# Splitting two loads of x so that the last store of a one-core attention-and-MLP kernel takes another DMA semaphore

## Chip, cores, metric

The kernel runs on one core of one Trainium2 chip. The metric is the device time of one execution in microseconds (us). The experiments e1 to e4 ran on one chip, e5 to e8 on another, each beside the kernel before.

## The reference, cut to what matters

```python
def reference(x, state, moe_w_in, moe_w_out):          # x [8,8,512,64], state [8,8,32,64]
    scores = 0.125 * x @ state^T;  xread = softmax(scores) @ state
    scores2 = 0.125 * state @ x^T; sread = softmax(scores2) @ x
    t = concat([xread, sread], axis=2) -> [4352, 512]  # 8 batches of 544 rows, heads side by side
    h = t @ moe_w_in                                   # 512 -> 2048
    return (h * sigmoid(h)) @ moe_w_out                # 2048 -> 512, float32
```

## The kernel before

x comes in batch by batch into two buffers in turn. x(4) to x(7) are loaded on the SP queue in the main loop, one load of 1 MB each, long before they are used:

```python
    def load_x(b, h0=0, nh=H, eng=nc.gpsimd):
        eng.dma_start(
            x_f[b % 2][:, ds(h0, nh)],
            x[b, ds(h0, nh)].rearrange("h (p c) d -> p h c d", p=128, c=4)
        )
    # ...
    for b in range(1, B):
        n = b + 1
        m = n + 1
        # ...
                if m + 1 < B:
                    if at == (0, 2):
                        load_x(m + 1, eng=nc.sync)
                    if at == (1, 0):
                        for c in range(4):
                            cast_x(m + 1, nc.gpsimd, c, 1)
                    if at == (2, 10):
                        transpose_x(m + 1)
```

The last 128 rows to be computed are written in pieces, so that the last one is small:

```python
    def last_cols(b, tt, f, n, eng, queue):
        # ... sixteen matmuls into ps, then
        o = opool.tile([128, n], FP32, tag=f"o_part{f}", name="o_part")
        copy(eng, o[:], ps[:, 0:n])
        queue.dma_start(out_sread[ds(512, 32), ds(4 * tt, 4), cols], o[:])
    # ...
    last_cols(B, 1, 0, 256, nc.scalar, nc.sync)
    last_cols(B, 1, 256, 128, nc.vector, nc.scalar)
    last_cols(B, 1, 384, 128, nc.vector, nc.sync)
```

What the source does not show: the framework gives the DMAs issued by SP and ScalarE eight semaphores in turn, HW0 to HW7, in program order. At the end of the program SP checks all of them, one instruction after the other, in a fixed order. In the built program of the kernel before that end reads so (SW0 to SW7 are the semaphores of GpSimd's DMAs; what each check waits for is in brackets):

```
check SW7, SW6
check HW0, SW5
check HW1, SW4
check HW2, SW3        [128 rows x 512, last but three]
check HW3, SW2        [last piece, columns 0-255]
check HW4, SW1        [last piece, columns 256-383, issued by ScalarE]
check HW5, SW0        [last piece, columns 384-511: the very last store]
check HW6, VectorE
check HW7, ScalarE
drain (GpSimd)
drain, barrier of all engines (twice), end
```

The softmax here doesn't subtract the row's maximum and nothing guards it: scores larger than these inputs give would overflow.

## Time and profile before

| | kernel before |
|---|---|
| time, median of three | 212.74 us (212.74 to 212.76) |
| profiled execution: time, span of its records | 213.31 us, 211.54 us |
| TensorE busy | 203.7 us, 96% |
| last store: issued, landed (last of the 16 increments of its semaphore) | 208.605, 210.505 us |
| from that landing to the end of the span | 1.035 us |

The span ends with the last record; the time is longer than the span by a nearly constant 1.77 to 1.82 us in the profiled executions compared here. The profiled execution is slower by 0.57 us than the three that were timed. To see where in the span time lies, take three stretches: up to 18.75 us, then 189.50 us up to the end of the matmuls, then the rest. The view of busy time by stretches, kernel before (columns: stretch, its length, then busy us and count of instructions for TensorE, its weight loads, VectorE, ScalarE and GpSimd, then granted clock, DMA share, GB/s):

```profile
0.00:18.75 18.75, 15.83 (x122) 6.99 (x124) 10.32 (x29) 11.37 (x23) 13.12 (x25) 1.00 1.07 198
18.75:208.25 189.50, 187.91 (x1430) 89.83 (x1451) 63.52 (x116) 127.98 (x221) 26.93 (x38) 1.00 0.51 130
208.25:211.54 3.29, 0.00 (x0) 0.00 (x0) 0.29 (x1) 0.00 (x0) 0.00 (x0) 1.00 0.22 69
```

TensorE fills the long middle. In the last 3.29 us no engine computes but VectorE for 0.29 us: there the time is copy, store, landing and the end of the program.

### The profile page before, as it was taken

To read this page: it belongs to the slowest core of one execution; us is meant where nothing else is said; L and a number is where in the kernel's file an instruction comes from. 1 tells how busy PE (TensorE), PEld (TensorE's weight loads), DVE (VectorE), ACT (ScalarE), POOL (GpSimd) and SP (SyncE) were. 2 spreads that over 40 slices of the span, in tenths; PEclk is the share of its full clock that TensorE was granted. 3 is DMA by queue.
4 is the path that set the end of the run, shared out by engine and by line. 5 is a ranking of instruction groups with operands and counts; after the bars stand their busy time and mean duration, and the time that the engine had idled before them with its cause. 6 is when DMAs were issued, how large, how long until landed. Compare 5 with 4: busy or idle time off the path is not lost.

```text
span 211.5 us, 3841 instructions
## 1 busy us (share of the span) xinstructions
PE 203.7 (96%) x1550; PEld 96.8 (46%) x1575; DVE 74.1 (35%) x146; ACT 139.3 (66%) x244; POOL 40.1 (19%) x62
## 2 busy tenths in 40 slices
PE   7799999999999999999999999999999999999993
PEld 2444454444444444444444444444444444466653
DVE  3842257657841236113410653043412306100011
ACT  3866677899577867697569855996775166644410
POOL 8672215503320042012201202000200000000000
PEclk9999999999999999999999999999999999999999
DMA  6999999995549756555935429114221111011112
GB/s 196 193 203 207 287 258 340 226 272 179 103 104 239 205 130 138 122 176 102 233 80 183 104 64 207 50 53 99 80 69 37 63 64 53 0 50 50 53 50 99
DMA packets 42929, 28.65 MB, mean 135 GB/s; under 512 B 28064, under 2 KB 37792, under 8 KB 42912
## 3 DMA queue, kind: packets, MB, share of 16 engines
q1 hardware_dynamic: 36720, 20.65, 37.4%
q0 software_dynamic: 5904, 7.64, 17.4%
q8 instruction: 12, 0.20, 0.4%
q10 hardware_dynamic: 288, 0.13, 0.2%
q14 instruction: 5, 0.04, 0.1%
HBM read 17.43 MB, written 8.91 MB: 125 GB/s over the span
## 4 chain that ended last, share of the span: by engine, by line
PE 90%; DMA 5%; POOL 2%; issue 1%; DVE 0%; POOLq 0%
PE o L566 50%; PE h L525 25%; DMA w_in_sb<-in_moe_w_in_dram 5%; PE ps_w L469 4%; PE h L546 3%; PE o_a L566 3%; PE o_part L588 2%; PE ps_sr L416 1%; PE ps_scT L332 1%; POOL w_in_sb L150 1%; POOL w_out_sb L153 1%; PE ps_sc L306 0%; PE ps_xt L253 0%; DVE W L159 0%; POOL st_n L191 0%
## 5 line engine op out<-in xcount | busy, mean ns | idle before, releaser
L566 PE MATMUL o<-w_out_sb,g 128*128 128x512 bf16 x480 | 129.5, 379 | 1.3 <-issue 0.5
L557 ACT ACTIVATE g<-h 128x512 bf16<-128x512 f32 (+1 forms) x143 | 81.3, 573 | 34.1 <-PE h L525 19.9
L566 PEld LDWEIGHTS <-g 128*128 128x128 bf16 x528 | 50.3, 98 | 59.1 <-issue 3.8
L525 PE MATMUL h<-aT,W 128*128 128x512 bf16 x247 | 73.1, 379 | 0.1
L159 DVE COPY o_sb<-o 128x512 f32<-128x512 f32 x15 | 10.4, 691 | 89.1 <-PE o L566 86.2
L525 PEld LDWEIGHTS <-W 128*128 128x128 bf16 x254 | 24.5, 98 | 30.3 <-issue 0.7
L159 DVE CAST W<-ps_w 128x512 bf16<-128x512 f32 (+2 forms) x36 | 22.2, 658 | 23.2 <-PE ps_w L469 23.2
L157 ACT ACTIVATE W<-ps_w 128x512 bf16<-128x512 f32 (+1 forms) x32 | 16.2, 562 | 11.1 <-PE ps_w L469 11.1
L159 POOL CAST x_nat<-x_f 128x512 bf16<-128x512 f32 x24 | 14.7, 655 | 35.7 <-DMA x_f<-in_x_dram 35.7
L157 ACT ACTIVATE o_sb<-o 128x512 f32<-128x512 f32 x16 | 9.5, 597 | 14.4 <-PE o L566 11.9
L362 POOL TENSOR_TENSOR an<-e,rcn 128x512 bf16<-128x512 bf16 x5 | 7.6, 1517 | 48.0 <-DVE rcn L360 48.0
L469 PE MATMUL ps_w<-w_in_sb,stT 64*32 64x512 bf16 (+2 forms) x264 | 10.3, 373 | 0.6 <-DMA w_in_sb<-in_moe_w_in_dram 0.6
L566 PE MATMUL o_a<-w_out_sb,g 128*128 128x512 bf16 x31 | 9.8, 379 | 0.2
L546 PE MATMUL h<-xmT,w_in_sb 128*128 128x256 bf16 x64 | 9.6, 273 | 0.1
L546 PEld LDWEIGHTS <-w_in_sb 128*128 128x128 bf16 x64 | 6.3, 98 | 3.9
L359 DVE TENSOR_REDUCE rs<-e 128x32 f32<-128x1024 bf16 x5 | 6.1, 1213 | 3.1 <-DMA e<-eT 3.1
L165 PE MATMUL ps_busy<-busy 128*128 128x512 bf16 x15 | 5.9, 497 | 1.2 <-DVE warm L172 1.2
L346 ACT ACTIVATE eT<-ps_scT 128x512 bf16<-128x512 f32 x10 | 5.4, 597 | 1.6 <-PE ps_scT L332 1.6
L786 ACT ACT_TABLE_LOAD x5 | 6.4, 1283 | 0.1
L469 PEld LDWEIGHTS <-stT 64*32 64x32 bf16 x264 | 3.2, 90 | 6.0 <-issue 4.1
L382 POOL TENSOR_TENSOR an<-exp_nat,rc 128x512 bf16<-128x512 bf16 x3 | 3.1, 1048 | 14.8 <-DVE rc L380 14.8
L768 ACT ACT_TABLE_LOAD x4 | 5.1, 1283 | 0.1
(76 smaller groups left out, 99.7 us busy)
## 6 DMA issues: line engine op xcount, KB each, us to landing
out_dram<-o_sb SPq DMA_DIRECT2D x33, 256.0 KB, 2.5
x_f<-in_x_dram SPq DMA_DIRECT2D x4, 1024.0 KB, 6.1
x_f<-in_x_dram POOLq DMA_DIRECT2D x2, 1024.0 KB, 11.9
w_in_sb<-in_moe_w_in_dram POOLq DMA_DIRECT2D x3, 512.0 KB, 10.5
x_f<-in_x_dram SPq DMA_DIRECT2D x2, 512.0 KB, 4.7
w_out_sb<-in_moe_w_out_dram POOLq DMA_DIRECT2D x4, 256.0 KB, 12.0
w_out_sb<-in_moe_w_out_dram POOLq DMA_DIRECT2D x2, 512.0 KB, 12.2
x_f<-in_x_dram POOLq DMA_DIRECT2D x2, 512.0 KB, 15.2
```

The source lines that it names most:

```text
L157: nc.scalar.activation(dst, src, func=COPY, bias=0.0)
L159: eng.tensor_copy(dst, src)
L165: nc.tensor.matmul(ps[:], busy[:, 0:128], busy[:], start=True, stop=True, skip_group_check=True)
L346: nc.scalar.activation(t[:, hg], scT_ps[hg][:], func=EXP, bias=0.0, scale=SCALE)
L359: nc.vector.tensor_reduce(rs[:], e2[b][:], axis=AX, op=ADD)
L362: eng.tensor_tensor(a[:, hg], e2[b][:, hg], rc[:, hg].to_broadcast([128, 4, 4, NS]), op=MULT)
L469: nc.tensor.matmul(pss[f, hg][ds(32 * s, 32), 0:n], stT[ds(r, 64), b, h // 2, s % 2, :], w_in_sb[ds(r, 64), h // 2, ds(f, n)], start=True, ...
L525: nc.tensor.matmul(h_ps[k][:], W1[b][:, hg, ds(128 * ft, 128)], aT[b][:, hg, :, :], start=(hg == 0), stop=(hg == 1), skip_group_check=True,)
L546: nc.tensor.matmul(ps[:, 0:256], w_in_sb[:, kt, ds(128 * ft, 128)], xmT[:, :, kt].rearrange("p t n b -> p t (n b)"), start=(kt == 0), stop ...
L557: nc.scalar.activation(g[:, 0:n], ps[:, 0:n], func=SILU, bias=0.0)
L566: nc.tensor.matmul(outs[tt][:], gt[b * NFT + ft][:, ds(128 * tt, 128)], w_out_sb[:, ft, :], start=(ft == 0), stop=(ft == NFT - 1), skip_gr ...
L786: nc.scalar.activation(warm[:], busy[:, 0:1], func=SILU, bias=0.0)
```

## The change

The intent is in the checks above. The two checks after HW5 were satisfied long ago, but stand behind the one that waits, so they are paid for after the landing. Two more DMAs anywhere earlier on SP or ScalarE move the last store on to HW7, the check that comes last. They are had by cutting two loads of x in halves.

```diff
                 if m + 1 < B:
                     if at == (0, 2):
-                        load_x(m + 1, eng=nc.sync)
+                        for h in range(0, H, 4 if b < 3 else H):
+                            load_x(m + 1, h, 4 if b < 3 else H, nc.sync)
```

## The prediction

> **What bounds the kernel now.** I read the page's busy shares first, then the chain that ended last, then the end of the program by itself, because the change aims at the end.
>
> ```profile
> PE 203.7 (96%) x1550; PEld 96.8 (46%) x1575; DVE 74.1 (35%) x146; ACT 139.3 (66%) x244; POOL 40.1 (19%) x62
> ...
> PE 90%; DMA 5%; POOL 2%; issue 1%; DVE 0%; POOLq 0%
> ```
>
> TensorE is busy for 203.7 of 211.5 us and makes up 90% of the chain of work. Anything that neither adds matmuls, nor makes TensorE wait, nor lies before its first or after its last matmul is worth nothing. The waits of TensorE say how little it waits for others (columns: engine, line, releaser, then us in total, times, longest):
>
> ```profile
> PE ps_busy L165 <- DVE warm L172: 1.2, 1, 1.2
> PE ps_w L469 <- DMA w_in_sb<-in_moe_w_in_dram: 0.6, 1, 0.6
> PE o L566 <- issue: 0.5, 3, 0.2
> ```
>
> No load of x to be split is among these. The end is different. The timeline from 206 us on, for the engines that still have work (columns: start us, us, engine, line, operation, tiles, count), and the line of the program's end on the SP queue in the stretch 210.5 to 210.75 us:
>
> ```profile
> 207.39 0.29 DVE L159 COPY o_part<-o_part 128x128 f32<-128x128 f32 x1 [5.40 <-PE o_part L588]
> 207.72 0.63 ACTq L598 DMA_DIRECT2D out_dram<-o_part  x1
> 208.29 0.29 DVE L159 COPY o_part<-o_part 128x128 f32<-128x128 f32 x1 [0.60 <-PE o_part L588]
> ```
>
> ```profile
> 208.60 0.54 SPq L598 DMA_DIRECT2D out_dram<-o_part  x1
> ```
>
> ```profile
> L839 SPq EVENT_SEMAPHORE  x3: 28/28/28, 210.5 to 210.6; - x3
> L839 SPq DRAIN  x1: 7/7/7, 210.7 to 210.7; - x1
> ```
>
> The last piece of output is copied by VectorE at 208.29 and stored by SP at 208.60. The store is issued in 0.54 us, but it has landed only when its semaphore has its 16 increments; the trace's records of that semaphore run from 210.352 to 210.505 us. Then SP has three checks left to make, and a drain. The exact starts in the trace are 210.522, 210.581 and 210.642 for the checks and 210.707 for the drain. Only after it comes SP's drain that joins the barrier of all engines (210.771), and from there to the end at 211.54 us it is two rounds of barrier, the same whatever was stored.
>
> Why three: in the built program the DMAs issued by SP and ScalarE take eight semaphores in turn, HW0 to HW7, and the end of the program checks them in that order, one instruction each (the first of the nine checks is for software queues alone). Before, the last four stores sit on HW2, HW3, HW4 and HW5. So the check of HW5 is the one that waits for the last store, and the checks of HW6 and HW7 follow it, both of which have long been satisfied (their last DMAs landed at 186.7 and 192.8 us).
>
> SP is the last at the barrier. The other engines' first drains in the same place are at 207.1 (TensorE, 1.195 us long), 208.3 and 208.4 us, more than two us before SP's. So a nanosecond off SP's tail is a nanosecond off the program.
>
> **What the Trainium skill says.** "Advanced Engine Details and Errata", section Network/Comms, gives 50 to 100 ns for reading a semaphore value from a sequencer. The trace agrees: the checks that had nothing to wait for start 59 to 69 ns apart (210.522, 210.581, 210.642; earlier 209.190, 209.259, 209.321, 209.385, 209.447). "Perfetto Trace Analysis", Identifying Dependency Chains, says that an instruction with waits on several engines may get EventSemaphore instructions put before it; this is the row of nine at the end. "DMA: Bandwidth & Descriptors", section Why a DMA increments its semaphore by 16 and not by 1, says that only the full 16 means that all has landed; here the check that waited started at 210.522, 17 ns after the sixteenth increment. The same page puts most of a DMA's fixed cost into the receipt of the write, not into the issue; the trace agrees, since the last store needs 1.9 us from issue to landing for 64 KB.
>
> **The change, part by part.** The loads of x(4) and x(5) on the SP queue (issued at 44.5 and 66.3 us) are each split in two of four heads. The loads of x(6) and x(7) stay whole.
>
> *Added.* Two more DMA issues on SP and one more event wait on GpSimd ahead of the cast of x(4), by the order of the built programs. One of today's whole loads costs SP 0.53 and 0.39 us to issue. I take the same again for a second half: 0.4 to 0.6 us each, one us in all, on a queue that after the first load stands waiting from 45.1 to 49.06 and after the second from 66.7 to 72.72 us for the next store's tile. Cost on the path: 0. The bytes and the contiguous rows (1 KB) are the same, so the transfers' time is the same but for one fixed cost, which lies beside the other half.
>
> *What waits for the halves.* GpSimd's casts take slices of all heads, so they wait for both. Of the stretches of each load:
>
> ```profile
> L109 SPq DMA_DIRECT2D x_f<-in_x_dram x1: 390/390/390, 66.3 to 66.3; - x1
> ...
> DMA to landing us min/median/max: 7.3/7.3/7.3
> ```
>
> ```profile
> 73.70 2.74 POOL L159 CAST x_nat<-x_f 128x512 bf16<-128x512 f32 x4 [11.78 <-DMA x_f<-in_x_dram]
> ```
>
> ```profile
> 77.75 2.05 SPq L144 DMA_TRANSPOSE xT<-x_nat  x1
> ```
>
> The second load lands at 73.55 and the cast runs from 73.70 to 76.44. The transpose that reads it starts at 77.75, held by a store ahead of it in the queue, which waited for ScalarE until 77.32. So there is 1.3 us of room before a late half would move even the transpose, and its result is read by TensorE only a block later. The first load lands at 50.36, and its cast starts at 51.85, behind GpSimd's other work, and its transpose at 61.40: room again. A 0.06 us check more on GpSimd there is inside it.
>
> *Moved.* All DMAs after the second split take a semaphore two further on. Each DMA waits for the DMA eight before it, in both kernels; following each such wait to the DMA that it names, I find none in the new program that is issued less than eight DMAs earlier, and the engines' waits name the same transfers as before apart from one wait of TensorE that falls away (for a transpose that had landed long before; worth nothing) and one pair on ScalarE that is grouped otherwise. TensorE, VectorE and ScalarE keep the number and order of their instructions.
>
> *Removed from the path.* The last four stores now take HW4, HW5, HW6 (the one from ScalarE) and HW7. The check of HW7 is the last. After the landing there is one check and the drain, where there were three checks and the drain. The gain is the two steps 210.522 to 210.581 and 210.581 to 210.642: 59 + 61 = 120 ns. The checks of HW0 to HW6 are made while the last store is in flight: SP is free at 209.14, the eight checks ahead of HW7's start some 62 ns apart from 209.19 on, so the eighth, HW6's, is reached at about 209.63 and waits for the second last store to land at 209.72. All are done by about 209.85, well before 210.5.
>
> Sum: 0 for the loads, 0 for the shift, -0.12 at the end. 212.74 - 0.12 = 212.62 us, that is -0.06%.
>
> **Rivals.**
> 1. *A half lands late.* If the two halves of x(5) queued behind each other and the second landed over 1.3 us later than 73.55, the transpose, and the store and the next transpose behind it in SP's queue, would move by the excess. For: this load already takes 7.3 us where another took 5.8. Against: 1 MB of the same rows goes through the same 16 engines, and the second half is issued only some 0.5 us after the first. Even then TensorE has a block (some 21 us) before it needs xT. It would leave 212.6, and at the worst, with TensorE held for a us, 213.6.
> 2. *The wait that was removed is replaced.* The barrier might be held by another engine, or the drain might wait for something that the two extra checks hid. Against: all other engines are at the barrier two us early, and the drain's own wait is for GpSimd, whose last work ended at about 150 us. It would make the gain 0: 212.74.
> 3. *The last store itself shifts.* Its time from issue to landing was 1.9 us, the two others of its kind 2.0 and 2.1. The gain is about as large as that spread. If TensorE's schedule or the landing moves by some tens of ns through the disturbed middle, the gain may be doubled or lost: 212.5 to 212.75. For: the write's receipt is outside the kernel's control. Against: three runs lie within 0.02 us, so the same program lands the same way; and nothing else moves DMA data in the last 2 us but the other two stores, whose spacing is kept.
>
> **Range and chances.** The centre is the sum, 212.62. The low end takes rival 3 in its good direction with another 0.2 us: 212.42. The high end is no gain with a little loss: 212.78. Two per cent is 4.25 us, 35 times what is at stake and more than the worst I can make of rival 1, so within 2% gets 0.98, and the rest is split evenly.
>
> **What would show it right or wrong.** Right: in the profile after, at the program's end on SP, one check and the drain behind the last landing, about 65 ns from that check to the drain, and the span near 211.42; the last store still issued at about 208.6 and landed about 1.9 us later. The chain of work still 90% TensorE, with four issues of x_f of 512 KB on SP in place of two of 1024 KB; the transposes at 61.4 and 77.75 where they were. Wrong: a new wait of TensorE for xT or for a store's tile near 50 to 90 us (rival 1); the last store issued earlier or later than 208.6 by over 0.05 us (the middle was disturbed); an end that comes as late after the landing as before, 1.03 us (rival 2); or a landing that takes 0.1 us longer or shorter (rival 3).

## The result, and the profile after

The ratio of two kernels is the mean time of the one's fast runs over that of the other's fast runs of the same rounds, so it is not quite the ratio of the medians. First comparison: the change 212.71 us median (212.61 to 212.88, six runs), before 212.84 (212.74 to 213.74, six runs, the first three among them); ratio 0.9987, 95% interval 0.9970 to 1.0004. That is inside the predicted range, and the interval contains 1: by the clock alone the gain is not shown.

The profile shows it. The page of the kernel after, its line of busy shares and its chain by engine:

```profile
PE 206.0 (98%) x1575; PEld 97.1 (46%) x1575; DVE 73.6 (35%) x146; ACT 139.2 (66%) x244; POOL 39.5 (19%) x62
...
PE 97%; DVE 1%; ACT 0%; issue 0%
```

TensorE's 206.0 us against 203.7 is no more work: both programs have the same matmuls, and the profile of before holds records of 1550 of the 1575. Counts have to be compared before busy times are. The line of the program's end on SP in the kernel after, in the stretch from 210.0 to 210.2 us, around the landing at 210.088:

```profile
L840 SPq EVENT_SEMAPHORE  x1: 28/28/28, 210.1 to 210.1; - x1
L840 SPq DRAIN  x1: 7/7/7, 210.2 to 210.2; - x1
```

One check and the drain where there were three and the drain. The same three stretches of the kernel after, begun at the same matmul (its weight load starts at 18.335 us here and at 18.751 before):

```profile
0.00:18.33 18.33, 16.58 (x123) 7.33 (x124) 10.04 (x29) 11.26 (x23) 12.71 (x24) 1.00 1.09 201
18.33:207.83 189.50, 189.44 (x1453) 89.75 (x1451) 63.28 (x116) 127.99 (x221) 26.77 (x38) 1.00 0.51 131
207.83:210.99 3.16, 0.00 (x1) 0.00 (x0) 0.29 (x1) 0.00 (x0) 0.00 (x0) 0.99 0.23 72
```

So the two spans differ by 211.540 - 210.992 = 0.548 us, and it lies in two places: 0.416 us before 18.75 us, and 0.131 us after the landing of the last store (1.035 us against 0.904). In between, TensorE's last weight load comes 189.223 us after that first one in both, to the nanosecond; the last store takes 1.900 us from issue to landing in both.

The 0.416 us at the start come before the first instruction that the change altered, which runs at 43.6 us. The waits of TensorE show one cause: before, it waited 0.6 us for w_in (in the prediction's second view); after, only these are left.

```profile
PE ps_busy L165 <- DVE warm L172: 1.2, 1, 1.2
PE ps_sc L306 <- DVE xT L159: 0.3, 1, 0.3
```

The first load of w_in, issued by GpSimd at 1.55 us in both, shows the time to landing in its line's view, before and then after:

```profile
DMA to landing us min/median/max: 6.7/6.7/6.7
```

```profile
DMA to landing us min/median/max: 5.3/5.3/5.3
```

The profile of before is of an execution in which the first weights came 1.4 us late. Whether that is chance or somehow the change's doing is a matter for experiments.

What the halves did to the queue, kernel after: the timeline on SP and on GpSimd, to be set against those at 66.27 and 73.70 us in the prediction.

```profile
64.92 1.01 SPq L109 DMA_DIRECT2D x_f<-in_x_dram  x2
```

```profile
71.65 2.28 POOL L159 CAST x_nat<-x_f 128x512 bf16<-128x512 f32 x4 [10.70 <-DMA x_f<-in_x_dram]
```

Two issues take 1.01 us in place of one of 0.39. The cast starts 2.0 us earlier than before, but that is not shown to be the halves' doing: executions differ by nearly as much by themselves. SP reaches this load at 65.88 us in the kernel before when it is run again (e1 below) and at 65.36 in the change when it is run again (e7), since the transposes ahead in its queue take from 1.2 to 2.5 us, and in e2, where this load is whole, the cast starts at 71.70 us, 5.8 us after the issue, sooner than behind the two halves here (6.7 us). TensorE's middle is the same to 9 ns (the table below), so all that is absorbed.

### The profile page after: what moved, and what is told of

The parts are those of the page before. It is cut to its first block, busy times and chain, and to the rows that moved or that the text cites. A ratio compares the mean times of both kernels' runs of the same rounds, so it can differ in the third digit from the quotient of the medians.

```text
span 211.0 us, 3869 instructions
## 1 busy us (share of the span) xinstructions
PE 206.0 (98%) x1575; PEld 97.1 (46%) x1575; DVE 73.6 (35%) x146; ACT 139.2 (66%) x244; POOL 39.5 (19%) x62
## 4 chain that ended last, share of the span: by engine, by line
PE 97%; DVE 1%; ACT 0%; issue 0%
PE o L566 51%; PE h L525 26%; PE ps_w L469 4%; PE h L546 3%; PE o_a L566 3%; PE ps_busy L165 3%; PE o_part L588 2%; PE ps_sr L416 1%; PE ps_xt L253 1%; PE ps_sc L306 1%; PE ps_scT L332 1%; PE ps_at L398 0%; DVE W L159 0%; ACT xT L157 0%; PE h L507 0%
## 5 line engine op out<-in xcount | busy, mean ns | idle before, releaser
L566 PE MATMUL o<-w_out_sb,g 128*128 128x512 bf16 x496 | 132.0, 379 | 0.0
L525 PE MATMUL h<-aT,W 128*128 128x512 bf16 x254 | 74.6, 379 | 0.1
L159 POOL CAST x_nat<-x_f 128x512 bf16<-128x512 f32 x24 | 14.2, 631 | 34.5 <-issue 22.6
L165 PE MATMUL ps_busy<-busy 128*128 128x512 bf16 x16 | 6.4, 520 | 1.2 <-DVE warm L172 1.2
```

Of the source, the lines that this page charges most:

```text
L159: eng.tensor_copy(dst, src)
L165: nc.tensor.matmul(ps[:], busy[:, 0:128], busy[:], start=True, stop=True, skip_group_check=True)
L525: nc.tensor.matmul(h_ps[k][:], W1[b][:, hg, ds(128 * ft, 128)], aT[b][:, hg, :, :], start=(hg == 0), stop=(hg == 1), skip_group_check=True,)
L566: nc.tensor.matmul(outs[tt][:], gt[b * NFT + ft][:, ds(128 * tt, 128)], w_out_sb[:, ft, :], start=(ft == 0), stop=(ft == NFT - 1), skip_gr ...
```

## The experiments

My theory: after the last landing, SP pays some 60 ns for every check that stands behind the one that waited, and nothing else of the change counts. Rivals: the halves of x gain (or cost) by themselves; the last store itself lands otherwise on another semaphore; the change took away the late start. Each kernel was profiled and timed five times. All results were correct. The edits of e2, e3, e5 and e8 are shown against the change, those of e4 and e6 against the kernel before.

### e1: the kernel before once more

No edit.

> The kernel before, unchanged, to see what the times and the profile do by themselves. From the last landing to the end of the span: 1.03 us again (before: 1.035; after the change: 0.904). My theory (only the two checks count, the rest of the difference of the two profiles is chance): the wait of TensorE for w_in of 0.6 us at the start of the profile of before is not there every time, so that this span may lie anywhere from 211.0 to 211.6 us; ratio to before 1.000 with an interval of 0.001 to 0.002. Rival (the change also took away something at the start): the wait is there again, the span is 211.5.

Measured: 213.04 us median (212.77 to 213.34) against 212.85 for the same kernel's nine other runs of that session (212.73 to 213.29), ratio 1.0007 (0.9995 to 1.0020). So the comparison of a kernel with itself can be off by 0.07%, half of what was measured for the change. The end of the program, right after the landing at 210.205:

```profile
L839 SPq EVENT_SEMAPHORE  x3: 28/28/28, 210.2 to 210.3; - x3
L839 SPq DRAIN  x1: 7/7/7, 210.4 to 210.4; - x1
```

Three checks again; 0.202 us from landing to drain, as before, and 1.025 to the end. The wait for w_in is gone, and the first load landed at 6.92 us instead of 8.26. Its span, 211.23, is 0.31 us under the first profile's, all of it from the start but 0.01. So the late w_in was that one execution's (no other of the ten profiles has this wait), and the rival that ascribed it to the change falls.

### e2: one load split

```diff
-                        for h in range(0, H, 4 if b < 3 else H):
-                            load_x(m + 1, h, 4 if b < 3 else H, nc.sync)
+                        for h in range(0, H, 4 if b < 2 else H):
+                            load_x(m + 1, h, 4 if b < 2 else H, nc.sync)
```

> Only the first of the two loads is split, so the last store takes HW6, and one check follows it in place of two (before) or none (the change). Theory of the checks: from the last landing to the end 1.035 - 0.06 = 0.97 us; time about 0.06 us under before. Rival (the split of the loads itself gains, or the landing of the last store changed): no step of 60 ns in the tail, 1.03 or 0.90 us.

Measured: two checks after the landing at 210.205, 0.143 us to the drain, 0.976 to the end. To the drain that is a step of 59 ns under before and of 62 over the change. Time 212.92 us (212.70 to 212.97), ratio 0.9999 (0.9986 to 1.0011): the clock cannot see 0.06 us.

```profile
L840 SPq EVENT_SEMAPHORE  x2: 28/28/28, 210.2 to 210.3; - x2
L840 SPq DRAIN  x1: 7/7/7, 210.3 to 210.3; - x1
```

### e3: three loads split

```diff
-                        for h in range(0, H, 4 if b < 3 else H):
-                            load_x(m + 1, h, 4 if b < 3 else H, nc.sync)
+                        for h in range(0, H, 4 if b < 4 else H):
+                            load_x(m + 1, h, 4 if b < 4 else H, nc.sync)
```

> Three loads are split, so the last store takes HW0, which is checked second of nine: seven checks follow the landing. Theory of the checks: from the last landing to the end 0.904 + 7 x 0.061 = 1.33 us, that is 0.43 us longer than the change and 0.30 longer than before, though more loads are split; time 213.04 if before gives 212.74. Rival (splitting loads is what gains): as fast as the change or faster, tail 0.90.

Measured: the landing at 209.930 is followed by eight checks, the waiting one and seven more:

```profile
L840 SPq EVENT_SEMAPHORE  x8: 28/28/28, 209.9 to 210.4; - x8
L840 SPq DRAIN  x1: 13/13/13, 210.4 to 210.4; - x1
```

Landing to drain 0.516 us, to the end 1.363 (1.33 expected; the checks here came 59 to 66 ns apart). Time 213.11 us (213.07 to 213.28), ratio to before 1.0011 (0.9997 to 1.0025), an interval that still contains 1. This is the sharpest test: the edit goes one step further in the direction of the change and turns the tail's gain of 0.13 us into a loss of 0.33. A gain from splitting as such would have grown.

### e4: the same shift without splitting

```diff
+    tinies = [pers.tile([16, 64], FP32, name=f"tiny{i}") for i in range(2)]
+
+    def tiny_load():
+        nc.sync.dma_start(tinies.pop()[:], state[0, 0, 0:16, :])
 ...
                         load_x(m + 1, eng=nc.sync)
+                        if b < 3:
+                            tiny_load()
```

> The loads stay whole; two loads of 4 KB that nobody reads are issued after them on the same queue instead, so that the semaphores move by two as in the change. Theory: the tail is that of the change, 0.90 us, and so is the time, 0.12 us under before. Rival (the halves of x landing earlier is part of the gain): tail 0.90 but TensorE's middle slower than the change, or the time that of before.

Measured, right after the landing at 210.196:

```profile
L845 SPq EVENT_SEMAPHORE  x1: 28/28/28, 210.2 to 210.2; - x1
L845 SPq DRAIN  x1: 7/7/7, 210.3 to 210.3; - x1
```

One check, 0.082 us to the drain, 0.905 to the end, which is the change's tail to the nanosecond or two, with whole loads. Time 212.89 us (212.62 to 213.41), ratio 1.0001 (0.9987 to 1.0014); its fastest run is 212.62. So far as the time goes this run alone decides nothing; its tail shows that the halves are not needed for the gain.

### e5: the split without the shift

The change, with six such tiny loads more, so that the semaphores come round to HW5 again:

```diff
                         for h in range(0, H, 4 if b < 3 else H):
                             load_x(m + 1, h, 4 if b < 3 else H, nc.sync)
+                        for _ in range(2 if b > 2 else 1):
+                            tiny_load()
```

> Both loads are split as in the change, and six loads of 4 KB that nobody reads are added on the same queue, so that the semaphores have gone round once and the last store is on HW5 again as before. Theory of the checks: the split alone is worth nothing; three checks after the landing, from it to the drain 0.202 us and to the end 1.03 us as in both runs of the kernel before, and from the issue of the first output store to that of the last 173.36 us as in all runs so far; time that of before. Rival (the split gains by itself): under 173.36 us in between, or a shorter tail.

Measured, right after the landing at 209.929:

```profile
L846 SPq EVENT_SEMAPHORE  x3: 28/28/28, 209.9 to 210.1; - x3
L846 SPq DRAIN  x1: 7/7/7, 210.1 to 210.1; - x1
```

Three checks, 0.203 us to the drain, 1.025 to the end, as in the kernel before; 173.36 us between the issues of the first and the last output store. Time 212.91 us (212.71 to 212.93), ratio 0.9996 (0.9983 to 1.0009). In the trace, the split alone is worth nothing.

### e6: the last store in halves, side by side

```diff
-        queue.dma_start(out_sread[ds(512, 32), ds(4 * tt, 4), cols], o[:])
+        if isinstance(queue, tuple):
+            for i, q in enumerate(queue):
+                q.dma_start(out_sread[ds(512 + 16 * i, 16), ds(4 * tt, 4), cols], o[ds(64 * i, 64), :])
+        else:
+            queue.dma_start(out_sread[ds(512, 32), ds(4 * tt, 4), cols], o[:])
 ...
-    last_cols(B, 1, 384, 128, nc.vector, nc.sync)
+    last_cols(B, 1, 384, 128, nc.vector, (nc.sync, nc.scalar))
```

(on top of e2, so that SP's half is on HW7)

> Not a test of the cause but a try at more: one load split, and the last store of 64 KB cut in two of 32 KB, issued by SP and ScalarE side by side, on HW7 and HW6. If the 0.54 us of issue are what a smaller store saves, each half lands some 0.2 us sooner and the span is 0.2 us under the change. If the two issues go one after the other, or the landing is receipt alone, it is the change's tail, 1.90 us from issue to landing, plus up to 0.06 us for a second check.

The timeline of this kernel at the last store:

```profile
208.03 0.57 SPq L600 DMA_DIRECT2D out_dram<-o_part  x1
208.03 0.58 ACTq L600 DMA_DIRECT2D out_dram<-o_part  x1
```

Half the rows did not shorten SP's issue (0.54 us for the whole). SP's half landed 1.825 us after its issue, ScalarE's 2.089: the later one counts, 0.19 us later than the whole store on SP did, and two checks come after it (0.991 us to the end). ScalarE's whole stores of 64 KB take as long (2.00 to 2.10 us in the eight profiles of the table below), so the half given to ScalarE gained nothing on them. Why its stores take longer is not shown: each was issued with another store still under way. Time 213.05 us (212.89 to 213.12), ratio 1.0006 (0.9992 to 1.0020). A miss.

### e7: the change once more

No edit to the change.

> The change, unchanged, once more beside before on one chip. Theory: one check after the landing, 0.081 us from landing to drain, 0.904 to the end; 173.36 us from the first output store's issue to the last one's; the time of all runs 0.12 us under before, which five rounds may not resolve, since runs of one kernel differ by some 0.3 us through the start. Rival (more than the checks is gained): time 0.28 us under before again, as in the first comparison.

Measured: 212.62 us median (212.60 to 213.10); four of five runs lie between 212.60 and 212.63. Before, in the same session: 213.03 median (212.72 to 214.41, ten runs); ratio 0.9990 (0.9977 to 1.0002). In the profile: one check, 0.081 us to the drain, 0.904 to the end, 173.36 us between the stores. The ratio is worth 0.21 us, about midway between 0.12 and the rival's 0.28, and its interval reaches from no gain to 0.5 us, so the times do not decide. The mean of before holds one run of 214.41 and several of 213.0 to 213.1, where the fastest three are 212.72, 212.72 and 212.73.

### e8: a narrower last piece

```diff
-    last_cols(B, 1, 256, 128, nc.vector, nc.scalar)
-    last_cols(B, 1, 384, 128, nc.vector, nc.sync)
+    last_cols(B, 1, 256, 192, nc.vector, nc.scalar)
+    last_cols(B, 1, 448, 64, nc.vector, nc.sync)
```

(on top of the change)

> The change with the last two pieces of 192 and 64 columns in place of 128 and 128: a copy and a store of half the size stand at the end, on HW7. If copy and store scale, the copy takes 0.07 us and the landing some 0.1 us less: span 0.15 us under the change. If sixteen matmuls of 64 columns cost as much as of 128 (their weight loads are the same), or the store of the 192 columns lands after the last, nothing is gained or 0.1 us lost.

Measured: the last copy took 0.226 us in place of 0.292, but the last store of half the bytes landed 1.960 us after its issue in place of 1.90, and the tail was 0.914 us. Time 212.77 us (212.57 to 212.82), ratio 0.9991 (0.9978 to 1.0003); its fastest run is 0.03 us under the change's, its median above that of e7. The two cancel; no run shows a version that clearly beats the change.

### The tails side by side

All times but the last column are from the trace's own records, which count in nanoseconds. "Checks" counts those made after the last landing, the waiting one with them. "Start" is the time of TensorE's weight load number 125, from which on its schedule was the same to 9 ns in all of these.

| kernel | semaphore of last store | checks | landing to drain, us | landing to end, us | issue to landing, us | first w_in landed, us | start, us | fastest run, us |
|---|---|---|---|---|---|---|---|---|
| before (first profile) | HW5 | 3 | 0.202 | 1.035 | 1.900 | 8.260 | 18.751 | 212.74 |
| e1, before again | HW5 | 3 | 0.202 | 1.025 | 1.904 | 6.916 | 18.443 | 212.77 |
| e5, split, no shift | HW5 | 3 | 0.203 | 1.025 | 1.897 | 6.859 | 18.175 | 212.71 |
| e2, one split | HW6 | 2 | 0.143 | 0.976 | 1.890 | 6.981 | 18.454 | 212.70 |
| change | HW7 | 1 | 0.081 | 0.904 | 1.900 | 6.816 | 18.335 | 212.61 |
| e7, change again | HW7 | 1 | 0.081 | 0.904 | 1.890 | 6.818 | 18.194 | 212.60 |
| e4, tiny loads, no split | HW7 | 1 | 0.082 | 0.905 | 1.893 | 6.970 | 18.449 | 212.62 |
| e3, three split | HW0 | 8 | 0.516 | 1.363 | 1.905 | 6.901 | 18.170 | 213.07 |

Landing to drain is a line in the number of checks: 0.081, 0.143, 0.202 and 0.516 us for 1, 2, 3 and 8, that is 59 to 63 ns a check. Nothing else after the start differs: from "start" to the end of the span it is 192.650 to 192.657 us with one check, 192.727 with two, 192.779 to 192.789 with three and 193.123 with eight, whatever was split. The fastest run of each kernel, taken as the one with the earliest start, follows: 212.60 to 212.62 with one check, 212.70 with two, 212.71 to 212.77 with three (212.72 the fastest of all other runs of before), 213.07 with eight. That reading rests on a choice, the fastest of five or so, and only the profiled executions show their start; it agrees with the tails.

## Why the prediction was right

The predicted 212.62 us came out as 212.71 and 212.62 (medians), inside 212.42 to 212.78 both times. That is in part luck: the range also holds 212.74, no gain at all, and e4, which has the change's tail, came out at 212.89, outside it, because runs start late or early by more than the gain. What bears the prediction out is its mechanism, read from the tails. By its steps:

- *TensorE bounds, and nothing of the change touches it.* Right: 189.223 us from the first common weight load to the last, before and after. The wait for w_in of 0.6 us that the prediction showed as part of the kernel was not: it was one execution's. For the size of the change it did not matter.
- *Two halves cost SP some 0.4 to 0.6 us each, off the path.* Right: 0.53 and 0.56 us for the first load, 0.39 and 0.53 for the second, and e5 has all of it at the time of before. The assumed room of 1.3 us was never used; the cast was done by 73.93 us, and its transpose started at 77.36.
- *The semaphores move by two, and no wait gets worse.* Right in effect: no new wait of TensorE, and e4, which moves them without a split, has the tail of the change.
- *Two checks of 59 and 61 ns leave the path: 120 ns.* Right: 121 ns from landing to drain. To the end of the span it is 121 to 131 ns, since the end after the drain varies by 10 ns between the two profiles of before.
- *The end near 211.42 us, the last store issued near 208.6.* Wrong, though not by the change: 210.99 and 208.19. I took the one profiled span as the kernel's own and subtracted from it. It was an execution with a late start, as its 213.31 us beside 212.74 could have told; the sum had rightly been taken from the timed runs. For the same reason other signs named beforehand missed: the last store came 0.42 us early, which was to mean a disturbed middle and did not; TensorE's share of the chain was 97%, not 90, since the chain no longer runs through the wait for w_in; and the first of the two transposes started at 60.25 us, not 61.4.
- *Rival 3, the landing of the last store shifts.* It did not: issue to landing took 1.890 to 1.905 us in all eight profiles of the table. The spread of 1.9 to 2.1 in the prediction was between stores of different queues and sizes, not between runs of one.
- *Rivals 1 and 2.* Neither showed: the second half of x(5) landed at 71.51 us, before the 73.55 of the whole load, and the end came 0.904 us after the landing, not 1.03.
- *Most of a DMA's fixed cost is the receipt of the write.* The prediction cites this from the page "DMA: Bandwidth & Descriptors", which breaks the cost down in its section Anatomy of one DMA, for GpSimd's path (this store is SP's), and took the 1.9 us from issue to landing for agreement. That sum says nothing of its parts. The trace's packets give them, for the last store of before: 0.54 us of issue, 0.66 from there to the first packet, 0.35 for the packets, and only 0.35 from the end of the last data packet to the landing. The other seven profiles of the table agree to 0.01 us. So here the larger part lies before the first packet, and the measurement decides. The sum of the prediction does not rest on it.

What stays open: why the first load of w_in lands at 8.26 us in one execution and at 6.8 to 7.0 in the others, and why the start spreads by another 0.28 us among those. One rival is not excluded. The three profiles without a split load (before, e1, e4) start at 18.44 us or later, the five with two or more split (the change, e3, e5, e7, e8) at 18.34 or earlier, and the two with one split are on both sides (18.45 in e2, 18.17 in e6). Ten profiles cannot tell whether the edit makes an early start more frequent, which would add to the gain in time. The kernel before has early starts too: its fastest run of 212.72 us leaves, by an estimate from its spans, 212.72 - 1.78 - 192.79 = 18.15 us for the start.

## What to carry to other kernels

When the framework closes a program with a row of waits in fixed order, what is paid is the waits that stand behind the last one to be satisfied, so it is worth arranging that the last transfer is waited on last; the gain is small (here 60 ns a place), and any later edit that adds or drops one DMA on these queues moves it again, up to a loss of 0.3 us at the wrong place. For an effect of a tenth of a us, read the stretch it acts on in the trace of several kernels with different doses, and don't trust the ratio of times: here a kernel against itself came out 0.07% apart, and two profiles differed three times as much through chance at the start as through the change at the end.

## What the Trainium skill lacked or had wrong

- "Advanced Engine Details and Errata", section Network/Comms, has 50 to 100 ns for reading a semaphore value from a sequencer. The runs agree (59 to 70 ns from one check to the next, though each check waits on two semaphores). What neither it nor another of the pages read here says is that such checks at a program's end stand in line behind the one that waits, so that the place of a transfer's semaphore in that row counts: 0.081 us from landing to drain with one check, 0.516 with eight.
- "DMA: Bandwidth & Descriptors", section Issuing engines are not separate DMA queues, says that issuing on several engines at once saves only the sequencers' time, and that this is usually small beside the DMA itself. For stores of this size it is not small: the issue took 0.54 of the 1.90 us to landing for the 64 KB, and in e6 0.57 of 1.83 us on SP and 0.58 of 2.09 on ScalarE for 32 KB each. What no page read here says is that a store of 64 KB took longer to land from ScalarE, with another store under way, (2.00 to 2.10 us) than from SP as the last store (1.89 to 1.91).
- On the receipt of the write, which the prediction cites from the same page, see the last point of the list in "Why the prediction was right": 0.35 of 1.90 us.
- No page read here speaks of how much a first load differs between executions of one program: the first load of w_in landed at 8.26 us in one execution of the kernel before and at 6.92 in another.
